# Two more staging places and two more places for decoded pieces of w_in, in memory that is not yet in use, with the order searched anew

## The chip, the core and the metric

The kernel runs on one core of a Trainium2 chip. The metric is the device time of one execution in microseconds (us). The engines are TensorE (PE, with its weight loads PEld), VectorE (DVE), ScalarE (ACT), GpSimd (POOL) and SyncE (SP), which here only issues DMAs.

## What is computed

An attention with two parts, and behind it a gated feed-forward layer. There are 8 batches, 8 heads, 576 positions of 64 values.

```
q_d, k_d, v_d = mean of 4 neighbouring positions          # 144 positions
x  = softmax(q_d k_d^T / 8) v_d, each row repeated 4 times
   + softmax(q k^T / 8 where |i - j| < 4, else -1e9) v    # a band
x  = heads side by side: 576 x 512 per batch
h  = relu(x @ w_in);  u, v = h[:, :512], h[:, 512:]       # w_in 512 x 1024
v  = (v - mean) / sqrt(var + 1e-6)
vs = w_spatial @ v + b_spatial                            # 576 x 576
out = (u * vs) @ w_out                                    # w_out 512 x 512
```

The inputs q, k, v, w_spatial and b_spatial are float32; w_in and w_out come as 64-bit floats.

## The kernel before

**How the work is tiled.** Heads go in pairs, 4 pairs per batch and 32 in all; `attention(n)` issues the steps of one pair, `gated(b)` those of one batch's feed-forward part. The steps have short names that the prediction uses. S: the banded scores of a pair (L748), on ten windows of 64 queries; the mask is added either by a product on PE ahead of it (L741) or on DVE (L761). Sd: the scores of the coarse attention (L810), of sums over 4 positions that DVE or POOL make (L720, L723). T and Td: both probabilities turned over on PE (L844, L891). AV and AVd: the products with v (L952, L919). Then DVE adds the two (tile xf, L971, L973), ACT rounds the sum to 16 bits (x high, L1002) and DVE stores what is left (x low, L1004). Between these, DVE takes the maxima (L764, L770; coarse L852 to L854), subtracts them (L767, L776) or scales them for ACT to subtract (L780), and adds up and inverts the sums (L794 to L801, L862, L866); ACT takes the exponentials. Which engine takes a step that could go to two is set by strings of letters, one letter per pair (`ON`).

V is x @ w_in's second half (L1029, the last 64 positions L1034), for five pieces of 128 positions: ACT applies the relu, DVE the statistics and the scaling, and the result is stored as a high and a low half in the tile vh. U is w_in's first half turned (L1092): eight pieces per batch, four for positions 0 to 255 and four for the rest. SP (not to be mixed up with the engine) is the product with w_spatial (L1124), also eight pieces; DVE multiplies each with its U (the gate, L1145) and the product is stored as high and low half in a tile of the tag g (L1130, L1135), of which there are three, ga and two in gb. O is the product with w_out (L1160, L1175). Every float32 operand of these products is a sum of two 16-bit halves, so each product takes three passes.

**The weights.** w_in and w_out come in eight and four pieces of 128 rows x 512 numbers of 64 bits, 512 KB each (L522). A piece is staged as it came in a place of the tag stg (four places, two in the tile stg, which lies where gb will be, two in more), decoded to float32 by ACT (L539) and DVE (L542, L547) into a place of the tag mb (six places), measured by ACT (L648), and, when all pieces of a matrix half are measured and the common scale is known (L479 to L503), split into two 16-bit halves by ACT (L510) and DVE (L513). WV is w_in's second half, WU its first. A place is free again when its last reader has run.

**What sets the order.** Nothing here is scheduled by hand. All steps are collected as operations with an engine, an assumed duration and the tiles that they read, write or hold; `Plan.run` then plays the program through and takes, at each step, the engine that could start first and on it the operation of the smallest rank among those that can start within `NEAR` of the first. The rank is the pair's or batch's number plus an offset from the tables `RANK`, `MRANK` and `WRANK`. The tables, `NEAR`, `STAY`, `EVICT` and the strings of `ON` are thus what the order hangs on. Each engine then runs its instructions in that order. Where the played time has a hole on PE in the first 110 us, filler matmuls are put in (L1204), which keep PE's clock up and whose result nobody reads.

Of the kernel before, what the change touches and what calls it, by code (L numbers as in the profile page):

```python
# [252 lines left out]
RANK = {"load": [143.005, 47.751, 252.982, -69.47, -172.22, -274.786, 560.411, -758.364, -311.459, 313.434, 266.06, 380.575,  # L253
            943.336, 399.915],
        "vload": [391.404, 86.345, 272.249, 337.531, 429.684, -52.69, -370.895, -252.053],
        "vabs": [509.637, -1181.093, -217.316, 87.185, -457.776, 123.004, -794.489, 144.366],
        "tv": [-183.93, 240.18, 765.617, 930.011, 56.071, -19.127, -157.242, 125.859],
        "sum": [-115.268, 142.997, -94.455, -372.167, 362.55, -75.596, 306.456, 702.576, 1696.966, 425.169, -234.075, 705.288,
            -421.357, 223.437],
        "S": [-1061.927, -157.575, 379.809, -830.223, -915.099, 670.631, 141.564, -649.896, 467.386, 88.454, 513.148, 238.256,  # L260
            245.41, 202.772],
        "E": [-534.894, -339.729, -702.236, 21.188, 160.003, 471.872, 219.972, 899.326, -409.142, -823.461, -265.585, -479.069,
            -503.017, -440.633],
        "N": [231.109, -483.572, -754.504, 524.152, -141.085, 397.308, 1325.226, -80.846, -320.013, -220.077, -64.133, -498.673,
            700.859, -253.394],
        "T": [-347.227, -440.539, -1149.413, -139.403, 917.828, -1374.545, -1166.794, 234.909, 536.972, -105.532, -561.257,
            -49.343, -383.904, -24.157],
        "Sd": [-228.884, 341.247, -989.571, 12.731, -290.563, 65.584, -210.501, 584.996, 760.783, -156.288, -493.755, 182.161,
            -206.462, -81.893],
        "Nd": [20.186, -634.328, -625.655, -47.029, -1024.698, 6.919, -369.885, -166.975, -196.395, -51.441, 745.233, 26.68,  # L270
            590.548, 680.939],
        "Td": [226.557, -226.969, 765.057, -163.935, 412.294, -360.224, 842.794, -998.859, 11.321, 28.445, -152.942, 58.045,
            -1153.807, -259.463],
        "AVd": [377.528, -777.682, -319.581, 176.718, 599.105, 1049.442, -339.489, -191.118, -286.676, -150.229, -415.778,
            -182.501, -118.84, 141.634],
        "AV": [60.151, -170.544, -717.724, 720.142, -836.725, 275.504, 440.562, -339.226, -949.724, 57.757, -184.347, -239.42,
            -4.966, -560.047],
        "X": [49.462, -601.369, 382.04, -619.469, -420.239, 803.995, 16.415, -27.426, 201.671, 266.124, -288.114, 118.52,
            -424.608, -87.751]}
MRANK = {"V": [[-120.813, 103.137], [-373.166, -785.223], [-588.287, 86.439], [-457.053, -295.554], [-271.069, 53.075],  # L280
            [-161.929, 7.172], [-384.75, 67.584], [1.753, -86.54]],
        "U0": [[-381.018, 507.475], [-225.844, -398.15], [392.079, 353.99], [415.277, -261.891], [-69.09, -16.703], [-362.251,
            -497.795], [59.314, -190.411], [573.297, -308.684]],
        "S0": [[631.14, 127.639], [-206.013, -184.383], [299.174, 561.899], [-372.357, 30.262], [381.875, 239.103], [33.324,
            19.169], [-136.587, -125.569], [104.744, -531.737]],
        "U1": [[66.951, 205.966], [432.921, 80.243], [202.58, -320.842], [-584.875, -261.385], [85.111, -539.421], [-290.079,
            -515.53], [-73.151, -407.568], [-105.893, -362.577]],
        "O0": [[170.632, -34.982], [-172.469, 696.573], [159.95, -390.053], [-841.668, -359.026], [22.932, -667.87], [-349.956,
            231.605], [321.827, -73.48], [-54.093, -578.395]],
        "S1": [[-122.247, -1002.997], [272.521, 179.124], [-502.627, -34.942], [83.425, -28.324], [193.115, 251.294], [212.725,  # L290
            -514.576], [-0.655, 14.458], [254.101, -410.908]],
        "O1": [[-425.021, 297.386], [239.962, 469.652], [56.568, -208.235], [-194.872, 129.628], [-641.125, -6.104], [281.584,
            274.929], [184.644, 89.516], [19.298, 376.248]]}
EVICT = 456.633
WRANK = {"WV load": [31.22, -21.921, 242.309, 4.474],
        "WV decode": [350.543, -287.444, -567.367, 661.466],
        "WV bound": [-83.736, 162.235, 909.503, 36.755, -835.361],
        "WV split": [-201.598, 11.031, -341.826, -1007.43],
        "WU load": [-364.293, 427.826, 390.089, -59.831],
# [950 lines left out]
```

## Time and profile before

| | us |
|---|---|
| median of 3 runs | 579.53 |
| lowest and highest run | 578.91, 579.99 |
| the profiled execution | 580.97 |
| its span, first to last instruction | 579.1 |
| PE busy | 551.6 (95%) |
| DVE busy | 414.1 (72%) |
| ACT busy | 376.3 (65%) |
| POOL busy | 186.7 (32%) |
| HBM read, written | 46.57 MB, 9.44 MB |

The profile gives a start and a duration for each instruction, and for each idle time what ended it. Neighbours on an engine overlap a little, so that what one instruction costs in a row of them is the distance of two starts, 0.05 to 0.1 us less than its duration. A stretch of the span is read by how busy each engine is in it; the mean over the span hides that.

### The profile page before, as it was taken

What the parts mean: (1) busy time and instruction counts of PE and PEld (TensorE: products, weight loads), DVE (VectorE), ACT (ScalarE), POOL (GpSimd) and SP (SyncE); (2) the same over time, 40 slices, a digit from 0 to 9 for tenths busy, and PEclk for the clock granted to TensorE, in tenths of its full rate; (3) what the DMA queues carried; (4) which work ended last, traced back from release to release, by engine and by line L of the source; (5) the groups of instructions that cost most, each with busy time, mean ns of one, the idle gap of its engine ahead of it and who ended that gap; (6) DMA issues with size and microseconds to landing.
All of it is one profiled execution on the core that took longest, in us unless ns stands there. A gap on an engine that the chain in (4) does not pass through costs nothing.

```text
span 579.1 us, 16048 instructions
## 1 busy us (share of the span) xinstructions
PE 551.6 (95%) x6501; PEld 368.0 (64%) x6501; DVE 414.1 (72%) x1084; ACT 376.3 (65%) x1076; POOL 186.7 (32%) x213
## 2 busy tenths in 40 slices
PE   5877899999999998999999999999999999999996
PEld 2445547764786566765776747778567567756752
DVE  5989899964898888578687776781976666844420
ACT  3689999457577677567575877565756665954422
POOL 3636533023531254154330432422422352202100
PEclk9999999999999999999999999999999999999999
DMA  8987870035322344225303343214220400010012
GB/s 285 338 241 213 215 180 1 1 102 143 88 83 91 115 103 126 65 90 138 86 20 119 99 113 102 84 65 108 77 100 2 138 2 19 8 32 1 20 54 74
DMA packets 37390, 57.04 MB, mean 99 GB/s; under 512 B 3650, under 2 KB 24130, under 8 KB 37316
## 3 DMA queue, kind: packets, MB, share of 16 engines
q1 hardware_dynamic: 35012, 48.94, 26.7%
q0 software_dynamic: 2304, 7.08, 7.2%
q8 instruction: 51, 0.84, 0.6%
q14 instruction: 23, 0.19, 0.1%
HBM read 46.57 MB, written 9.44 MB: 97 GB/s over the span
## 4 chain that ended last, share of the span: by engine, by line
PE 70%; DVE 18%; ACT 6%; issue 2%; DMA 2%; POOL 0%; SPq 0%; ACTq 0%; DVEq 0%; POOLq 0%
PE pmd L1124 4%; PE pma L1124 4%; PE pmb L1160 4%; PE pma L1160 4%; PE pmc L1029 4%; PE pmc L1160 4%; PE pma L1029 4%; PE pmc L1124 3%; PE pmb L1124 3%; PE pmd L1029 3%; PE pmd L1092 2%; PE pma L1092 2%; PE pmc L1092 2%; PE pmb L1029 2%; PE pmd L1160 2%
## 5 line engine op out<-in xcount | busy, mean ns | idle before, releaser
L1092 PEld LDWEIGHTS <-win 128*128 128x128 f16 x768 | 74.7, 98 | 20.8 <-issue 0.6
L1124 PEld LDWEIGHTS <-vha 128*128 128x128 f16 x768 | 74.0, 98 | 20.6 <-issue 2.1
L1160 PEld LDWEIGHTS <-gb 128*128 128x128 f16 x264 | 25.6, 98 | 28.5 <-issue 0.4
L1124 PE MATMUL pma<-wsp,vha 128*128 128x256 f16 (+1 forms) x216 | 29.4, 286 | 0.0
L1124 PE MATMUL pmd<-wsp,vha 128*128 128x256 f16 (+1 forms) x204 | 27.6, 285 | 1.3 <-DVE aua L1105 1.3
L1204 PE MATMUL pma<-mask_b,mask_a 128*128 128x512 bf16 x83 | 23.4, 415 | 3.1 <-DVE mask_a L383 3.1
L1124 PE MATMUL pmb<-wsp,vha 128*128 128x256 f16 (+1 forms) x180 | 24.1, 283 | 0.0
L1124 PE MATMUL pmc<-wsp,vha 128*128 128x320 f16 (+1 forms) x168 | 23.5, 290 | 0.0
L1160 PE MATMUL pmb<-wo,gb 128*128 128x512 f16 x96 | 22.0, 379 | 0.0
L1160 PEld LDWEIGHTS <-ga 128*128 128x128 f16 x120 | 11.6, 98 | 12.8 <-issue 0.2
L1057 POOL TENSOR_TENSOR sta<-sta,mhalf 128x1 f32<-128x1 f32 (+1 forms) x14 | 9.0, 646 | 32.3 <-DVE sta L1041 32.3
L669 POOL DMA_DIRECT2D tvb<-v_dram x12 | 10.8, 900 | 18.2 <-DMA tvb<-v_dram 15.7
L1160 PE MATMUL pma<-wo,gb 128*128 128x512 f16 x72 | 16.5, 379 | 0.0
L1029 PEld LDWEIGHTS <-xa 128*128 128x128 f16 x96 | 9.2, 98 | 10.8 <-issue 0.2
L1204 PEld LDWEIGHTS <-mask_a 128*128 128x128 bf16 x85 | 7.9, 104 | 12.6 <-issue 3.7
L720 POOL TENSOR_TENSOR suma<-qka 128x576 f32<-128x576 f32 x6 | 7.8, 1294 | 23.4 <-DMA qka<-qk_dram 23.4
L669 POOL DMA_DIRECT2D tva<-v_dram x12 | 10.8, 902 | 13.2 <-DMA tva<-v_dram 8.9
L1057 POOL TENSOR_TENSOR stb<-stb,mhalf 128x1 f32<-128x1 f32 (+1 forms) x15 | 10.9, 725 | 11.4 <-DVE stb L1041 11.4
L1160 PE MATMUL pmc<-wo,gb 128*128 128x512 f16 x60 | 13.8, 379 | 0.0
L1057 POOL TENSOR_TENSOR stc<-stc,mhalf 128x1 f32<-128x1 f32 (+1 forms) x11 | 7.5, 678 | 18.7 <-DVE stc L1041 15.2
L720 POOL TENSOR_TENSOR sumb<-qkb 128x576 f32<-128x576 f32 x6 | 7.8, 1296 | 16.5 <-DMA qkb<-qk_dram 16.5
L862 POOL TENSOR_SCALAR smdb<-smdb 112x3 f32<-112x3 f32 x3 | 0.6, 201 | 38.6 <-ACT eda L858 38.6
(1085 smaller groups left out, 1725.7 us busy)
## 6 DMA issues: line engine op xcount, KB each, us to landing
qka<-qk_dram SPq DMA_DIRECT2D x15, 576.0 KB, 4.9
qkb<-qk_dram SPq DMA_DIRECT2D x15, 576.0 KB, 6.2
tva<-v_dram POOLq DMA_DIRECT2D x12, 288.0 KB, 5.5
tvb<-v_dram POOLq DMA_DIRECT2D x12, 288.0 KB, 4.3
stg<-w_in_dram SPq DMA_DIRECT2D x5, 512.0 KB, 8.3
out_dram<-rowc SPq DMA_DIRECT2D x7, 256.0 KB, 2.2
out_dram<-rowb SPq DMA_DIRECT2D x7, 256.0 KB, 2.0
out_dram<-rowe SPq DMA_DIRECT2D x7, 256.0 KB, 2.1
```

The costliest lines, as they stand in the source:

```text
L669: plan.op("POOL", 850, lambda r=r: nc.gpsimd.dma_start(t.ap[LOW:KEYS], v4[b, r], accum_op=ALU.add), w=[t], rank=rank + 2.0 + 0.3 * r, kb=2 ...
L720: side(s1).tensor_tensor(sb.ap.rearrange("p x (g r) -> p x g r", r=2), x[:, :, :, :2], x[:, :, :, 2:], op=ALU.add)
L862: side(ivd).tensor_scalar(smd.ap[:PD], smd.ap[:PD], 1.0e-9, 4.0, op0=ALU.add, op1=ALU.mult)
L1029: nc.tensor.matmul(ps.ap, xs[c].ap[:, i, t * P:(t + 1) * P], win[:, c, j, FF:], start=(c == 0 and (i, j) == (0, 0)), stop=(c == NC - 1 and ...
L1057: plan.op("POOL", 530, lambda: nc.gpsimd.tensor_tensor(st.ap[:r, 8:9], st.ap[:r, 8:9], mhalf[:r], op=ALU.pow), w=[st], rank=rank - EVICT, ...
L1092: nc.tensor.matmul(ps.ap[:, :n], win[:, c, i, ft * P:(ft + 1) * P], xs[c].ap[:, j, HA[h]:HA[h + 1]], start=(c == 0 and (i, j) == (0, 0)), ...
L1124: nc.tensor.matmul(ps.ap[:, :n], vh.ap[:, c, i, fs], wsp[:, c, j, hs], start=(c == 0 and (i, j) == (0, 0)), stop=False)
L1160: nc.tensor.matmul(ps.ap, g.ap[:, c, HA[1] * i + k:HA[1] * i + k + P], wo[:, c, j, :], start=(c == 0 and (i, j) == (0, 0)), stop=(c == NF ...
L1204: nc.tensor.matmul(ap.rearrange("p (j k) -> p j k", k=64), mask_a, mask_b[:, None, :].broadcast_to([P, 8, 64]), start=True, stop=True)
```

## The change

Two tiles are added in memory that is used for something else later. `extra` (two staging places, tag stv) lies where vh, the normalised v, will be; the first two pieces of WU are staged there. `spare` (two places for decoded pieces, tag mbx) lies where ga, the first gated tile, will be; the last two pieces of WU are decoded into it. vh and ga are made when they are first needed, as gb already was. So w_in's eight pieces have six staging places and eight places for their decoded form. Two conditions follow: V of the first batch waits for all that use the places of stv, and the first SP for all that use those of mbx. All tables of the order have new numbers.

```diff
-RANK = {"load": [143.005, 47.751, 252.982, -69.47, -172.22, -274.786, 560.411, -758.364, -311.459, 313.434, 266.06, 380.575,
+RANK = {"load": [193.743, 24.538, 296.961, -103.771, 2.185, -58.429, 515.387, -691.613, -313.739, 439.058, 82.64, 215.719,
...
-NEAR = 104.496
-STAY = 26.882
+NEAR = 101.451
+STAY = 32.658
...
-ON = {"sub": "DDDDDDADDADAAADDDADDAAADDDA",
+ON = {"sub": "AADDDDAAAAADAAADDADAADAADDDDDDAD",
...
-        "mask": "TTTTTTTTD",
-        "norm": "PDPPPDPDPPDDDPDPPPDPDPDPPPPDDPD",
+        "mask": "DTTTTTTDTD",
+        "norm": "PDPPPDPPDDPDPPPDPDDDDDPDDPPDDDPD",
...
-    plan.tag("g", [const.tile([P, NF, 2 * HA[1]], F16, name="ga"), g_place(0), g_place(1)])
+    spare = const.tile([P, 2, FF], F32, tag="ga", name="spare")
+    plan.tag("mbx", [spare[:, 0], spare[:, 1]])
+    plan.tag("g", [lambda: const.tile([P, NF, 2 * HA[1]], F16, tag="ga", name="ga"), g_place(0), g_place(1)])
...
-    places("vh", 1, [P, NT, 2, FF], F16)
+    extra = const.tile([P, 2, 2 * FF], F32, tag="vh", name="extra")
+    plan.tag("stv", [extra[:, 0], extra[:, 1]])
+    plan.tag("vh", [lambda: const.tile([P, NT, 2, FF], F16, tag="vh", name="vha")])
...
-        t = fetch([(src, 0)], key, 1600)
-        eb, mb = plan.buf("row"), plan.buf("mb")
+        t = fetch([(src, 0)], key, 1600, "stv" if key in (("WU", 0), ("WU", 1)) else "stg")
+        eb, mb = plan.buf("row"), plan.buf("mbx" if key in (("WU", 2), ("WU", 3)) else "mb")
...
+    def users(tag):
+        return [o for o in weights if any(b.tag == tag for b in o.bufs)]
...
-                plan.op("PE", 12 * 216, mm, r=xr + wtok["WV"], w=[ps], hold=[vr, vh], rank=rank, lag=PEL + 60, mode="F", name="V")
+                plan.op("PE", 12 * 216, mm, r=xr + wtok["WV"], w=[ps], hold=[vr, vh], after=users("stv") if b == 0 else (), rank=rank, lag=PEL + 60, mode="F", name="V")
...
-            first = weights if (b, h) in ((0, 1), (1, 0)) else ()
+            first = weights if (b, h) in ((0, 1), (1, 0)) else users("mbx") if b == 0 else ()
```

What the numbers do to the order can be seen where the instructions stand. The line numbers of the new kernel are 3 to 8 higher.

SP's queue, the first DMAs of the program; `stg`, `more` and `extra` take pieces of w_in, `qka` to `qkd` the queries and keys of the first four pairs, `tva` the coarse v. Before:

```order
L667 DMA tva<-v_dram 72x1024
L522 DMA stg<-w_in_dram 128x1024 x2
L713 DMA qka<-qk_dram 128x1152
L713 DMA qkb<-qk_dram 128x1152
L522 DMA more<-w_in_dram 128x1024 x2
L713 DMA qkc<-qk_dram 128x1152
L713 DMA qkd<-qk_dram 128x1152
L522 DMA wsta<-wT_dram 128x576
L522 DMA biasa<-bsp_dram 2x576
```

In the new order:

```order
L526 DMA extra<-w_in_dram 128x1024
L674 DMA tva<-v_dram 72x1024
L526 DMA stg<-w_in_dram 128x1024 x2
L720 DMA qka<-qk_dram 128x1152
L720 DMA qkb<-qk_dram 128x1152
L526 DMA more<-w_in_dram 128x1024 x2
L720 DMA qkc<-qk_dram 128x1152
L720 DMA qkd<-qk_dram 128x1152
L526 DMA extra<-w_in_dram 128x1024
L526 DMA wsta<-wT_dram 128x576
```

One piece stands ahead of everything, another behind qkd; the four that came first stand as they did.

ACT's queue, where WU is split (`win<-mb...` and `win<-spare`; `xe` is the first x of the second batch, `edb` a coarse exponential, `rowd`, `rowa` and `rowc` are V's relu). Before:

```order
L1047 ACTIVATE rowd<-pmb,sx2a 128x512
L686 ACTIVATE junk,sxb<-va 128x640
L510 ACTIVATE win<-mbf,sw 128x512
L510 ACTIVATE win<-mbc,sw 128x512
L1047 ACTIVATE rowa<-pma,sx2a 128x512
L510 ACTIVATE win<-mbd,sw 128x512
L539 ACTIVATE rowe<-stg 128x512
L686 ACTIVATE junk,sxa<-vb 128x640
L1047 ACTIVATE rowc<-pmd,sx2a 128x512
L510 ACTIVATE win<-mbe,sw 128x512
L1002 ACTIVATE xe<-xfb,sxb 128x576
```

In the new order:

```order
L901 COPY pdTa<-pmc 100x288
L543 ACTIVATE rowc<-more 128x512
L514 ACTIVATE win<-mbf,sw 128x512
L514 ACTIVATE win<-mbe,sw 128x512
L865 ACTIVATE edb,smdb<-paa,mxdb 112x2x72
L865 ACTIVATE edb,smdb<-pmb,mxdb 112x2x72
L865 ACTIVATE edb,smdb<-paa,mxdb 112x2x72
L514 ACTIVATE win<-spare,sw 128x512 x2
L693 ACTIVATE junk,sxb<-ve 128x640
L853 COPY probTb<-paa 128x640
```

The four splits stood among the relus of V, so behind the first batch's last x; now they stand among the steps of the first batch's attention, ahead of every x.

DVE's queue at the last split of w_out (`wo<-mb...`; `uf`, `ug`, `uh` are gates of the first batch, `xf` its row sums of the second). Before:

```order
L836 TENSOR_TENSOR sb<-sb,smd 128x640
L513 SCALAR_TENSOR_TENSOR wo<-mbb,sw,wo 128x512
L513 SCALAR_TENSOR_TENSOR wo<-mba,sw,wo 128x512
L971 TENSOR_TENSOR xfa<-paa,dnb 128x2x116 x2
L973 TENSOR_TENSOR xfa<-paa,dnb 128x112
L482 TENSOR_REDUCE aua<-pmd 1x1
L483 TENSOR_SCALAR aua<-aua 1x1
L513 SCALAR_TENSOR_TENSOR wo<-mbf,sw,wo 128x512
L513 SCALAR_TENSOR_TENSOR wo<-mbc,sw,wo 128x512
L1004 SCALAR_TENSOR_TENSOR xf<-xfa,sxb,xf 128x576
```

In the new order:

```order
L859 TENSOR_REDUCE mxda<-pab 112x2
L860 TENSOR_REDUCE mxda<-pmc 112x1
L861 TENSOR_SCALAR mxda<-mxda 112x3
L1142 TENSOR_TENSOR ga<-uf,ga 128x256
L1152 SCALAR_TENSOR_TENSOR ug<-pmd,aua,ug 128x256
L517 SCALAR_TENSOR_TENSOR wo<-mbb,sw,wo 128x512
L801 TENSOR_REDUCE smd<-sc 128x10
L933 TENSOR_TENSOR dnb<-paa,dnb 128x144
L804 TENSOR_SCALAR smd<-smd 128x10
L808 RECIPROCAL smd<-smd 128x10
L1152 SCALAR_TENSOR_TENSOR uh<-pma,aua,uh 128x256
```

The four splits stood close together ahead of the first gate; the last one now stands behind two gates, with the steps of two pairs around it.

## Rows read from the trace of the kernel before

**Rows 1.** The busy time of each engine in six stretches of the whole program (stretch in us, its length, busy us and count of instructions by engine, granted clock, share of the DMA engines, GB/s).

```profile
0.00:12.91 12.91, 6.45 (x59) 2.77 (x59) 7.86 (x18) 3.94 (x7) 3.62 (x18) 1.00 0.84 269
12.91:40.93 28.02, 22.67 (x293) 12.86 (x297) 23.26 (x57) 18.77 (x55) 14.11 (x15) 0.94 0.95 287
40.93:72.42 31.49, 25.24 (x537) 16.61 (x527) 29.57 (x78) 30.55 (x88) 18.39 (x19) 1.00 0.82 229
72.42:106.17 33.75, 32.04 (x263) 20.83 (x262) 32.62 (x88) 30.16 (x73) 9.77 (x11) 1.00 0.32 78
106.17:134.40 28.23, 28.23 (x365) 18.93 (x365) 22.94 (x64) 15.35 (x45) 7.20 (x6) 1.00 0.28 90
134.40:579.10 444.70, 436.98 (x5002) 295.99 (x5000) 297.80 (x783) 277.55 (x812) 133.58 (x144) 1.00 0.27 75
```

**Rows 2.** The timeline of PE at the end of the program, its last matmuls (start, us, what, how many in a row).

```profile
571.36 2.75 PE L1175 MATMUL pmd<-wo,gta 128*128 128x512 f16 x12
```

**Rows 3.** The waits of PE from 72 to 575 us, the first and the last of seven (us in total, times, longest).

```profile
PE pmd L1124 <- DVE aua L1105: 1.3, 1, 1.3
...
PE pma L1092 <- DVE win L513: 0.2, 1, 0.2
```

**Rows 4.** The busy time of line 1204 alone (the filler matmuls) over stretches that make up the whole span, their sum.

```profile
sum 579.10, PE 24.04 PEld 7.94; mean PE 4.81 PEld 1.59
```

**Rows 5.** DVE in the first 106.17 us, its busy time and number of instructions, and two of its waits there, the longest behind the first decodes and the shortest of the eight.

```profile
0.00:106.17 106.17, 93.31 (x239) 0.98 0.70 201
...
DVE mxb L770 <- PE pab L748: 1.6, 1, 1.6
...
DVE sxa L482 <- PE pmb L479: 0.2, 1, 0.2
```

**Rows 6.** The chain of waits in the first 125 us (start, us, what).

```profile
2.59 10.28 DMA qkb<-qk_dram
...
104.00 1.32 DVE wo L513 x2
...
106.17 1.79 PE pmd L1124 x12
...
110.14 0.55 PE pab L844 x5
```

**Rows 7.** The timeline of ACT and, below it, of DVE in the first 80 us (start, us, line, out<-in).

```profile
5.84 0.66 ACT L539 ACTIVATE rowa<-stg 128x512 f32<-128x512 f32 x1 [3.82 <-DMA stg<-w_in_dram]
...
44.40 0.67 ACT L539 ACTIVATE rowb<-more 128x512 f32<-128x512 f32 x1
...
77.81 0.73 ACT L510 ACTIVATE win<-mbf,sw 128x512 f16<-128x512 f32 x1
...
9.67 0.75 DVE L720 TENSOR_TENSOR suma<-qka 128x576 f32<-128x576 f32 x1
...
40.93 0.74 DVE L513 SCALAR_TENSOR_TENSOR win<-mbd,sw,win 128x512 f16<-128x512 f32 x1
```

**Rows 8.** The timeline of PE, one masked block of scores in the opening and the five steps of one pair later on.

```profile
70.78 0.43 PE L741 MATMUL pab<-mask_b,mask_a 128*128 128x320 bf16 x2
...
209.03 0.72 PE L919 MATMUL pab<-pdTa,tvb 64*64 64x144 f32 x16
209.58 0.80 PE L952 MATMUL pab<-probTa,vf 64*64 64x60 f32 x38
...
211.45 0.49 PE L891 MATMUL pma<-perm,edb 112*100 112x112 f32 x3
...
212.07 0.49 PE L1092 MATMUL pmd<-xb,win 128*128 128x256 f16 x3
```

**Rows 9.** The timeline of DVE ahead of the second batch's V.

```profile
131.00 0.89 DVE L761 TENSOR_TENSOR sa<-pab,mask 128x384 f32<-128x384 f32 x2
131.92 0.82 DVE L764 TENSOR_REDUCE mxb<-sa 128x10 f32<-128x640 f32 x1
...
132.86 0.81 DVE L1004 SCALAR_TENSOR_TENSOR xa<-xfa,sxb,xa 128x576 f16<-128x576 f32 x1
133.58 0.45 DVE L852 TENSOR_REDUCE mxdb<-pab 112x2 f32<-112x288 f32 x1
...
134.28 0.17 DVE L854 TENSOR_SCALAR mxdb<-mxdb 112x3 f32<-112x3 f32 x1
```

**Rows 10.** Groups of DVE's instructions in the first 106.17 us (busy us, mean ns of one), and below them two rows of the timelines of DVE and POOL that overlap.

```profile
L720 DVE TENSOR_TENSOR suma<-qka 128x576 f32<-128x576 f32 x2 | 3.2, 1577 | 0.0
L542 DVE TENSOR_SCALAR mba<-rowa 128x512 int32<-128x512 int32 x2 | 1.9, 956 | 0.7 <-ACT rowa L539 0.7
L854 DVE TENSOR_SCALAR mxda<-mxda 112x3 f32<-112x3 f32 x2 | 1.8, 892 | 0.1
L513 DVE SCALAR_TENSOR_TENSOR wsp<-wstc,sw,wsp 128x576 f16<-128x576 f32 x1 | 1.7, 1705 | 0.0
...
L542 DVE TENSOR_SCALAR mbc<-rowc 128x512 int32<-128x512 int32 x2 | 0.8, 416 | 0.0
...
26.81 2.40 DVE L720 TENSOR_TENSOR suma<-qka 128x576 f32<-128x576 f32 x1
...
27.45 1.14 POOL L720 TENSOR_TENSOR sumb<-qkb 128x576 f32<-128x576 f32 x1
```

**Rows 11.** The timeline of PE at the first V of the second batch.

```profile
134.23 0.81 PE L1029 MATMUL pmc<-win,xe 128*128 128x512 f16 x3
```

More of the change, by code (lines that the diff above doesn't have):

```diff
@@ L247, in run @@
         return end
-RANK = {"load": [143.005, 47.751, 252.982, -69.47, -172.22, -274.786, 560.411, -758.364, -311.459, 313.434, 266.06, 380.575,
[L254 to L299, printed above, removed]
-        "WU decode": [387.574, -316.232, 1019.795, 459.568],
-        "WU bound": [1425.684, -228.293, 245.85, 118.051, 725.352],
-        "WU split": [-187.848, -607.313, -258.771, -328.661],
-        "WSP load": [289.708, -579.107, 622.627, -316.354, 744.76],
-        "WSP bound": [397.382, 106.669, -930.598, 200.751, 873.332, -382.338],
-        "WSP split": [-150.625, -91.686, 309.424, 430.824, -1165.74],
-        "WO load": [201.774, -325.888, 429.457, 987.307],
-        "WO decode": [137.835, 619.019, -225.889, -8.083],
-        "WO bound": [-64.148, 457.463, -289.1, 18.247, -58.582],
-        "WO split": [620.04, -563.746, 894.059, 1022.164]}
@@ new lines @@
+EVICT = 424.128
+WRANK = {"WV load": [8.932, -69.308, 237.335, -113.461],
+        "WV decode": [498.39, -173.71, -746.769, 879.963],
+        "WV bound": [75.164, 328.117, 1096.662, 290.394, -1001.895],
+        "WV split": [-246.43, 101.682, -127.118, -970.709],
+        "WU load": [-496.994, 344.788, 640.584, 37.355],
+        "WU decode": [469.162, -148.932, 1081.304, 729.559],
+        "WU bound": [1666.078, -368.299, 333.39, 481.782, 710.79],
+        "WU split": [-307.465, -783.187, -230.312, -132.514],
+        "WSP load": [481.299, -741.394, 761.131, -123.43, 725.764],
+        "WSP bound": [-211.952, 408.604, -994.87, 166.184, 872.953, -437.445],
+        "WSP split": [-58.134, -137.272, 55.809, 426.781, -1354.283],
+        "WO load": [130.61, -93.203, 516.501, 829.072],
+        "WO decode": [15.979, 664.366, -112.237, 34.148],
+        "WO bound": [-19.709, 334.246, -466.101, 68.581, 19.425],
+        "WO split": [888.478, -529.737, 813.101, 1132.568]}
@@ L320 @@
 UPN = 0
[L322 to L329 removed]
+ON = {"sub": "AADDDDAAAAADAAADDADAADAADDDDDDAD",
+        "inv": "DDDDDDPDDDPDPDDDDPDPDPDDDPDDPPD",
+        "invd": "DDDPDDDPDPPPDDDDDPPPDDPPPDPDDDPD",
+        "sum": "PPPPPDDDDPDDPPPDDPDPDDPPPPDDDDPD",
+        "mask": "DTTTTTTDTD",
+        "norm": "PDPPPDPPDDPDPPPDPDDDDDPDDPPDDDPD",
+        "normd": "PAAPDDAAAPAAPDDAPDADDDPADPDPAAAP",
+        "vlo": "DPDDPDDPDPDPDDDDPPDDPDPDDDPDPDPPDPDP"}
 @with_exitstack
```

45 lines of the change are left out of this document (40 added, 5 removed).

## The prediction, made before the changed kernel ran

> **What bounds the kernel now.** I read the page's 40 slices first, then the engines' busy time cut at five points, then the chain of waits, and at last single rows of VectorE (DVE) and TensorE (PE). The reader is to see two kernels in one. PE is busy nearly all the time, but the stretches differ [rows 1]: from 134.40 us to the end PE is busy 436.98 of 444.70 us, and 5.0 of the 7.7 us that are missing lie behind its last matmul [rows 2]; the waits of PE from 72 us on are seven, 1.3 us the longest and 4.2 us in sum [rows 3]. Before 72.42 us, where the first V (w_in times the first batch) starts, PE's busy time is 6.45 + 22.67 + 25.24 = 54.4 us, but 24.0 of these are filler matmuls that only keep PE awake [rows 4]. So of the first 72.4 us PE uses 30.3, and by 106.17 us, where the first gated product of the second half starts (SP of the tile called ue), it has used 86.4 - 24.0 = 62.4 and lost 43.8. After that it loses 2.5 us in four of those waits, and the tail. **The span is thus a fixed amount of PE work, 527.6 us, plus what PE loses before 106 us, 43.8, plus 7.7 us.** A new order can win or lose only by that second part, unless it opens holes behind it.
>
> What sets the second part is DVE, with ScalarE (ACT) close by. DVE is busy 93.31 of the first 106.17 us [rows 5]; of the 12.9 us that it idles, some 5 are the start and the first decodes, and eight waits behind them, 1.6 us the longest, make up 5.7. From 40.93 us, where the first split of w_in ends on ACT's side, it is busy 29.57 of 31.49 and 32.62 of 33.75 us [rows 1], and the chain runs through it up to 105 us [rows 6]: the last split of w_out (tile mbc) starts at 104.59 us there, and the SP that needs all weights starts at 106.17.
>
> **The change, part by part.** *Two staging places more.* In the new order the first DMA of SP's queue is a w_in piece (tile extra) in front of tva, stg, qka and qkb. A piece is 512 KB, and the core moves 269 GB/s in the first 12.9 us and 287 in the 28 us behind [rows 1]. So whatever stands behind it lands 512 KB / 287 to 269 GB/s = 1.8 to 1.9 us later: the first decode (5.84 us, after 3.82 us of waiting), and qkb, whose landing at 12.87 us opens the chain [rows 6, 7]. In return all eight w_in pieces are decoded before the third pair's scores are exponentiated; before, ACT decodes the seventh at 44.40 us [rows 7]. The bytes of the first 41 us are nearly the same, at a DMA share of 0.84 to 0.95 [rows 1], so a piece that goes early pushes another back.
>
> *Two decoded places more.* w_in's first half (for U) is bound and split before the first x is finished; before, that was done from 77.81 us on, beside the running V [rows 7]. In the new order four more splits stand ahead of the last x of the batch on DVE, each 0.74 us [rows 7]. That work is not saved, it is moved from a place where PE was saturated to a place where PE waits for DVE.
>
> *The two waits that come with it.* The first V waits until two staged pieces are decoded, the first SP until two decoded pieces are split. Both stand on DVE ahead of the last x of the batch, which V waits for anyway. Behind them on PE queue V, U and SP, but the price is nothing as long as the x come last; if that cover went, a split's 0.74 us would show [rows 7]. The filler matmuls go from 85 to 95 in the program; they run in holes and cost nothing, or 0.28 us each where one is in the way (24.04 us for 85) [rows 4].
>
> *The order.* I count DVE's and PE's work up to the same event in both kernels: the SP of ue, which must have the last w_out split. On PE the new order has done more by then: one S, Sd, AV and T and two Td and AVd more, and one mask product less. The pair at 209.03 us shows AVd, AV, S, Sd and Td in 212.07 - 209.03 = 3.04 us, Td takes 0.62 of them and AVd 0.55, T is 0.55 in the chain and a mask product 0.43 [rows 6, 8]: 3.04 + 0.55 + 0.62 + 0.55 - 0.4 = 4.4 us. This is no loss, it would be done later.
>
> On DVE the new order has done still more by the last w_out split. From start to start of the rows where they stand in line [rows 7, 9]: sums of two pairs more, 2 x (0.75 and, over half as many elements, 0.4) = 2.3; masks of two pairs that PE masked before, 2 x 0.9 = 1.8; one maximum more, 0.8; three pairs fewer whose maximum is subtracted on DVE (ACT's exponential does it now; like the mask it passes over all scores), -3 x 0.8 = -2.4, with four small scalings, +0.3; one more pair of coarse maxima, 0.8 (133.58 to 134.45), and of inverses, 0.7; one norm less and one coarse norm more, +0.2; one dn, xf and xlo more, 0.2 + 0.8 + 0.7 = 1.7; one v-low more, 0.6; the gate's scale, two gates and one low part before the last split instead of behind it, 1.6. What has no row of its own here I size by the rows of like form. Sum 8.4 us. The bounds: 7 if the small ones run beside others, 9.4 if they are slowed as often as before.
>
> So DVE is later by 8.4 us and PE by only 4.4 us of useful work: PE loses **4.0 us** more, if DVE idles as long as before. Does it? The opening is worse by the 1.8 us of the extra piece; the eight waits of DVE behind that, 5.7 us in sum [rows 5], can shrink, since more decoding stands ready to fill them. Stepping through the first 40 us by these rows I get the first w_in split about 1 us earlier with 1.1 us less work ahead of it: no gain in idle time. I take idle as unchanged and keep -5.7 and +1.8 as bounds. From the V on, the count by PE gives the same: by the last x, DVE has 2.4 us more to do (four splits, less a column reduction and some subtractions), PE has 4.0 us less behind it, of which 1 to 3 us can come back since U and V are now mixed; that is +3.4 to +6.4.
>
> Behind that point: the same PE work less one mask product (0.36), one round more of switches between attention and projections; I set this to nothing. The four waits of 2.5 us [rows 3] may go or come anew. The tail is alike: the last product, two copies, two stores.
>
> **Sum.** The profiled execution took 580.97 us with a span of 579.1; the median of the three runs is 579.53, 1.4 below it. Span 579.1 + 4.0 = 583.1, execution 585.0; against the median **583.5 us**.
>
> **Rivals.** (1) *DVE is held up less.* In the first 106 us some DVE rows take far longer than their like while GpSimd (POOL) runs: two sums of suma 3.2 us where one alone takes 0.75, two rows of mba 1.9 where mbc's take 0.8, two of mxda 1.8 where one can take 0.17, a split of wsp 1.7 where one of w_in takes 0.74 [rows 7, 9, 10]; 1.7 + 1.1 + 1.4 + 0.9 = 5.1 us together. The new order meets POOL otherwise. If none of them came back, DVE's 8.4 would be 3.3, and PE would lose 5.1 less than in my sum: 578.4. For it: by the order POOL has three normalisations fewer in all. Against: it has two sums more, and suma was hit by just such a sum. The Trainium skill, SBUF — State Buffer, "Who interferes with whom", says that a VectorE instruction with two SBUF inputs and a GpSimd instruction that reads SBUF take turns on one port, whichever starts first; by that rule the slow sum of suma (26.81 to 29.21 us) waits for POOL's sum at 27.45 to 28.59, and the trace agrees, since the two overlap and the DVE row ends 0.6 us behind the other [rows 10]. Chance of ending faster 0.12.
>
> (2) *The gaps are filled.* If the early decodes took all of the 5.7 us of DVE waits, less the 1.8 us of the late opening, DVE would be 3.9 us ahead of my sum: 579.6, no change. With one or two slowed rows fewer it is faster. Chance 0.23, a third of it faster.
>
> (3) *The second batch's V stalls* (slower still). Before, its last x is done at 133.67 us [rows 9] and V starts at 134.23 [rows 11]: nothing to spare. In the new order PE has 7.2 us less work ahead of that V (counted from the order as above), so it comes there at 134.2 - 7.2 + 4.0 = 131.0, while DVE has 1.1 us more work ahead of that x. DVE idles 28.23 - 22.94 = 5.3 us between 106 and 134 [rows 1]. If that idle time stays, the x is done at 134.8 and PE stalls 3.8 us more: 587.3. If it goes, x is done at 129.5 and nothing happens. It decides as long as less than all 3.8 us of that idle time goes. Against it: AV of that pair now stands 5.3 us of PE work ahead of the V, and the chain behind it took 3.8. Chance 0.20.
>
> (4) *The pieces come no earlier*, because DMA is full. Then the decodes wait on ACT in front of the exponentials, and the opening costs its 1.8 us as well: 585.3. It lies within my forecast's own range.
>
> **How the numbers follow.** My forecast (with 4) covers +1.2 to +6 us: 0.45. Rival 3: 0.20. Rivals 1 and 2 together 0.35, of which 0.20 faster and 0.15 within 0.2% (1.2 us, about what a measurement of this kernel can tell from no change). Faster 0.20, same 0.15, slower 0.65. The range reaches down past rival 1, 577.5, and up past rival 3, 588.0.
>
> **What would show it.** Right: the last w_out split some 8 us later than 104.6, the SP of ue at 114 to 116 us, DVE 95% busy between 41 and 112 us, PE without a hole from then on. The first V at 73 to 76 us with one pair's scores fewer done. Wrong: that SP before 111 us (DVE idles less or meets POOL less), or later holes in PE of more than 6 us, which would be the searched order's own and not this sum's.

## The result and the profile after

The changed kernel takes 583.7 us (median of 4 runs, 583.16 to 584.3) where the kernel before takes 579.7 in the same four rounds: ratio 1.0071, 95% interval 1.0054 to 1.0089, so 4 us slower. The profiled execution took 583.63 us, its span is 581.9.

The same six stretches as in [rows 1], of the kernel after:

```profile
0.00:12.91 12.91, 7.70 (x60) 3.07 (x60) 6.04 (x16) 3.95 (x7) 5.26 (x20) 1.00 0.85 280
12.91:40.93 28.02, 20.56 (x262) 11.65 (x263) 22.30 (x50) 21.01 (x72) 14.85 (x16) 0.94 0.92 291
40.93:72.42 31.49, 24.29 (x456) 15.23 (x457) 30.63 (x94) 30.13 (x84) 6.49 (x7) 1.00 0.78 213
72.42:106.17 33.75, 31.73 (x322) 20.31 (x322) 32.19 (x82) 31.37 (x80) 13.74 (x16) 1.00 0.37 85
106.17:134.40 28.23, 28.23 (x449) 20.77 (x441) 25.92 (x79) 21.58 (x77) 1.89 (x2) 1.00 0.30 95
134.40:581.90 447.50, 441.21 (x4977) 298.79 (x4975) 291.23 (x776) 269.24 (x770) 133.83 (x146) 1.00 0.26 74
```

The busy time of the filler matmuls alone (the line that is 1204 in [rows 4]), up to the first V and behind it, and their sum:

```profile
0.00:72.42 72.42, 26.02 (x95) 9.10 (x95) 0.98 0.84 255
72.42:581.90 509.48, 0.22 (x2) 0.00 (x0) 1.00 0.27 76
sum 581.90, PE 26.24 PEld 9.10; mean PE 13.12 PEld 4.55
```

The timeline of PE: the first V of the first batch, the SP of ue, the first V of the second batch ([rows 6, 11] have the last two before):

```profile
72.48 0.81 PE L1036 MATMUL pmb<-win,xa 128*128 128x512 f16 x3
...
115.71 1.79 PE L1131 MATMUL pmb<-wsp,vha 128*128 128x320 f16 x12
...
132.28 0.81 PE L1036 MATMUL pmd<-win,xe 128*128 128x512 f16 x3
```

The timeline of ACT in the opening, as in [rows 7]; line 543 is the first step of a decode, line 795 the exponential that ACT takes window by window:

```profile
7.89 0.66 ACT L543 ACTIVATE rowa<-stg 128x512 f32<-128x512 f32 x1 [5.88 <-DMA stg<-w_in_dram]
...
15.44 0.66 ACT L543 ACTIVATE rowc<-more 128x512 f32<-128x512 f32 x1 [3.40 <-DMA more<-w_in_dram]
16.00 2.48 ACT L795 ACTIVATE sa<-sa,mxa 128x64 f32<-128x64 f32 x10
18.51 2.16 ACT L795 ACTIVATE sb<-pab,mxb 128x64 f32<-128x64 f32 x10
...
30.03 0.69 ACT L543 ACTIVATE rowc<-stg 128x512 f32<-128x512 f32 x1
```

The timeline of DVE: a sum that is held up, the first w_in split, the last x of the batch, the last w_out split:

```profile
34.18 1.81 DVE L727 TENSOR_TENSOR sumb<-qkb 128x576 f32<-128x576 f32 x1
...
43.44 0.74 DVE L517 SCALAR_TENSOR_TENSOR win<-mbd,sw,win 128x512 f16<-128x512 f32 x1
...
72.26 0.81 DVE L1011 SCALAR_TENSOR_TENSOR xd<-xfa,sxa,xd 128x576 f16<-128x576 f32 x1
...
114.40 0.74 DVE L517 SCALAR_TENSOR_TENSOR wo<-mbb,sw,wo 128x512 f16<-128x512 f32 x1
```

DVE's waits up to there, the longest and two on these exponentials (us in total, times, longest):

```profile
DVE mba L546 <- ACT rowa L543: 2.8, 1, 2.8
...
DVE sma L801 <- ACT sa L795: 1.2, 1, 1.2
DVE smb L801 <- ACT sb L795: 1.2, 2, 0.7
```

POOL beside the sum that is held up:

```profile
34.06 1.32 POOL L843 TENSOR_TENSOR sa<-sa,sma 128x640 f32<-128x640 f32 x1 [2.14 <-DVE sma L808]
```

Busy time up to the end of the last w_out split (columns as above):

```profile
0.00:115.13 115.13, 93.23 (x1279) 57.54 (x1280) 99.28 (x262) 93.71 (x268) 42.22 (x59) 0.99 0.67 193
```

What to see. V starts where it did, 72.48 against 72.42 us, but PE has used only 52.55 - 26.02 = 26.5 us by then instead of 30.3: some 4 us of attention work are left for later. By the SP of ue (115.71 us, 9.5 later than in [rows 6]) PE has used 52.55 + 31.73 + 9.54 - 26.24 = 67.6 us and lost **48.1**, against 43.8 before. Behind that SP it loses 6.3 us where it lost 7.7, because the span is 581.9 and PE's useful work unchanged (553.71 - 26.24 = 527.5 us). Together +2.8 us of span; the rest of the 4 us is that the profiled execution of before lay 1.4 above its median, and this one does not.

### The profile page after: what moved, and what is told of

The parts are those of the page before. It is cut to its first block, busy times and chain, and to the rows that moved or that the text cites. A ratio compares the mean times of both kernels' runs of the same rounds, so it can differ in the third digit from the quotient of the medians.

```text
span 581.9 us, 16082 instructions
## 1 busy us (share of the span) xinstructions
PE 553.7 (95%) x6509; PEld 369.8 (64%) x6509; DVE 408.3 (70%) x1091; ACT 377.3 (65%) x1085; POOL 176.1 (30%) x205
## 4 chain that ended last, share of the span: by engine, by line
PE 76%; DVE 10%; ACT 7%; DMA 3%; issue 1%; SPq 1%; ACTq 0%; DVEq 0%
PE pmd L1131 5%; PE pma L1131 5%; PE pmd L1036 4%; PE pmc L1099 4%; PE pmd L1167 4%; PE pmb L1099 4%; PE pma L1099 4%; PE pma L1036 3%; PE pma L1167 3%; PE pmd L1099 3%; PE pmb L1131 3%; PE pmc L1131 3%; PE pmc L1167 3%; PE pmb L1036 3%; PE pmb L1167 2%; PE pmc L1036 2%
## 5 line engine op out<-in xcount | busy, mean ns | idle before, releaser
L1131 PE MATMUL pmd<-wsp,vha 128*128 128x256 f16 (+1 forms) x252 | 33.6, 283 | 0.4 <-ACT edb L865 0.4
L1131 PE MATMUL pma<-wsp,vha 128*128 128x320 f16 (+1 forms) x228 | 31.9, 289 | 0.0
L1131 PE MATMUL pmc<-wsp,vha 128*128 128x256 f16 (+1 forms) x144 | 19.6, 286 | 0.0
L1131 PE MATMUL pmb<-wsp,vha 128*128 128x320 f16 (+1 forms) x144 | 19.6, 286 | 0.0
L1167 PE MATMUL pmd<-wo,gb 128*128 128x512 f16 x84 | 19.3, 379 | 0.0
L1211 PEld LDWEIGHTS <-mask_a 128*128 128x128 bf16 x95 | 9.1, 105 | 14.5 <-issue 5.2
L1167 PE MATMUL pmc<-wo,gb 128*128 128x512 f16 x72 | 16.5, 379 | 0.0
L869 POOL TENSOR_SCALAR smdd<-smdd 112x3 f32<-112x3 f32 x5 | 1.3, 260 | 39.1 <-ACT edb L865 39.0
L1064 POOL TENSOR_TENSOR stb<-stb,mhalf 128x1 f32<-128x1 f32 (+1 forms) x12 | 8.9, 741 | 13.3 <-DVE stb L1048 11.2
L1045 DVE BATCH_NORM_STATS2 stc<-rowc 128x6 f32<-128x512 f32 x3 | 2.1, 693 | 13.4 <-ACT rowc L1054 13.4
## 6 DMA issues: line engine op xcount, KB each, us to landing
stg<-w_in_dram SPq DMA_DIRECT2D x4, 512.0 KB, 12.3
```

What stands on the lines that cost most here:

```text
L869: side(ivd).tensor_scalar(smd.ap[:PD], smd.ap[:PD], 1.0e-9, 4.0, op0=ALU.add, op1=ALU.mult)
L1045: nc.vector.bn_stats(st.ap[:r, :6], vr.ap[:r])
L1064: plan.op("POOL", 530, lambda: nc.gpsimd.tensor_tensor(st.ap[:r, 8:9], st.ap[:r, 8:9], mhalf[:r], op=ALU.pow), w=[st], rank=rank - EVICT, ...
L1131: nc.tensor.matmul(ps.ap[:, :n], vh.ap[:, c, i, fs], wsp[:, c, j, hs], start=(c == 0 and (i, j) == (0, 0)), stop=False)
L1167: nc.tensor.matmul(ps.ap, g.ap[:, c, HA[1] * i + k:HA[1] * i + k + P], wo[:, c, j, :], start=(c == 0 and (i, j) == (0, 0)), stop=(c == NF ...
L1211: nc.tensor.matmul(ap.rearrange("p (j k) -> p j k", k=64), mask_a, mask_b[:, None, :].broadcast_to([P, 8, 64]), start=True, stop=True)
```

## The experiments

In the runs on the order, one part of the new order is undone and every other instruction of every engine stays where it was, the fillers too. "V" is the start of the first V in the run's profiled execution, "behind V" that execution's time less V, "first split" the start of the first split of w_in on DVE. The medians, and the ratios to the kernel before in the same rounds (its median there lies between 579.47 and 579.84) with their 95% intervals:

| run | median us | ratio | first split | V | behind V |
|---|---|---|---|---|---|
| the kernel after | 583.70 | 1.0071 (1.0054 to 1.0089) | 43.44 | 72.48 | 511.2 |
| late_extra | 582.05 | 1.0038 (1.0023 to 1.0053) | 41.52 | 70.55 | 511.4 |
| no_exp_by_window | 582.92 | 1.0061 (1.0039 to 1.0082) | 41.98 | 71.01 | 511.8 |
| opening_both | 582.64 | 1.0047 (1.0035 to 1.0059) | 41.65 | 70.68 | 512.1 |
| no_splits | 582.19 | 1.0048 (1.0032 to 1.0064) | 43.12 | 70.86 | 512.0 |
| no_splits_late_extra | 581.06 | 1.0025 (1.0013 to 1.0036) | 41.67 | 69.42 | 511.6 |
| late_splits | 586.32 | 1.0109 (1.0091 to 1.0128) | 43.45 | 71.16 | 515.8 |
| splits_spread | 586.74 | 1.0114 (1.0098 to 1.0130) | 43.49 | 71.25 | 515.5 |
| all_three | 586.35 | 1.0107 (1.0092 to 1.0123) | 42.02 | 69.77 | 516.7 |
| the kernel before | 579.7 | 1 | 40.93 | 72.42 | 508.6 |
| places_alone | 579.44 | 0.9997 (0.9984 to 1.0011) | 39.42 | 70.88 | 508.5 |
| dve_price | 582.38 | 1.0047 (1.0034 to 1.0061) | 39.65 | 73.81 | 508.2 |
| act_price | 583.79 | 1.0064 (1.0040 to 1.0088) | 42.16 | 75.83 | 508.0 |
| dve_price_late | 585.48 | 1.0096 (1.0068 to 1.0124) | 39.08 | 70.56 | 512.6 |

From the first split to V the profiled executions repeat to 0.05 us: 31.46 to 31.49 us in the kernel before, places_alone and dve_price_late, 29.03 or 29.04 in the kernel after and the three runs below it in the table, 27.71 to 27.76 in the five runs without the four splits there. Ahead of it they do not. Four executions run the old order unchanged up to there (the kernel before, places_alone, dve_price, dve_price_late) and have it at 39.08 to 40.93 us. In three of them the granted clock falls to 0.50 on the way, in the kernel before from 14 to 16 us, in places_alone and dve_price from 28 to 30; in dve_price_late it stays at 1.00. So a difference of a microsecond or two in one execution's opening needs the medians beside it.

### places_alone: the new places in the old order

The diff is that of the change without its tables and letters.

> The new places and the two waits that come with them, but the order of the kernel before, instruction by instruction on every engine, with its letters and its filler matmuls. If the loss is the order's alone: as the kernel before, 579.7 us within 0.6. If the places or their waits cost something themselves: 581 us or more. If they give something by themselves (a DMA that no longer waits for a place): 578.5 or less.

579.44 us, no difference. The places, the tiles that are made late and the two added waits cost nothing and give nothing that can be told from zero (the interval is -0.9 to +0.6 us); the loss is the order's. The run shows one thing more. Its first w_in split, its first V and its SP of ue, in the old order, stand at (timelines of DVE and PE)

```profile
39.42 0.74 DVE L621 SCALAR_TENSOR_TENSOR win<-mbd,sw,win 128x512 f16<-128x512 f32 x1
...
70.88 0.82 PE L1140 MATMUL pmb<-win,xa 128*128 128x512 f16 x3
...
104.64 1.79 PE L1235 MATMUL pmd<-wsp,vha 128*128 128x320 f16 x12 [1.34 <-DVE aua L1216]
```

and dve_price_late, whose order up to V is also the old one, has V at 70.56. The profiled execution of before, with 72.42, was one with a late opening, by 1.5 to 1.9 us, about what it lies above its median. The delay arises early: the second pair's scores, which wait for qkb, start at 12.91 us there and run at a falling clock,

```profile
12.91 1.16 PE L748 MATMUL pab<-qkb 64*64 64x64 f32 x40 [2.07 <-DMA qkb<-qk_dram]
```

against 11.66 us and 0.81 for them in places_alone.

### late_extra: the extra piece later

```diff
 SP's queue
-L526 DMA extra<-w_in_dram 128x1024
 L674 DMA tva<-v_dram 72x1024
...
 L720 DMA qkd<-qk_dram 128x1152
+L526 DMA extra<-w_in_dram 128x1024
 L526 DMA extra<-w_in_dram 128x1024
```

> The changed kernel in its own order, with one edit: the first piece in the tile extra is issued on SP's queue behind qkd, next to the second one, instead of ahead of everything. Theory A (the extra piece delays the opening by the 1.8 us that it takes): first decode at about 6 us instead of 7.89, DVE idle of the first 25 us from 11.2 to about 9.4 us, time 581.9 us. Theory B (that idle time comes from the exponentials that ACT now takes window by window in the first two pairs): the opening's end does not move, 583.7 us within 0.5.

582.05 us, 1.65 less than the kernel after, as theory A had it. ACT's first decode starts at 5.34 instead of 7.89:

```profile
5.34 0.67 ACT L647 ACTIVATE rowa<-stg 128x512 f32<-128x512 f32 x1 [3.33 <-DMA stg<-w_in_dram]
```

and V starts 1.9 us earlier with the same work ahead of it, all of which is won ahead of the first w_in split:

```profile
41.52 0.74 DVE L621 SCALAR_TENSOR_TENSOR win<-mbd,sw,win 128x512 f16<-128x512 f32 x1
```

Other executions agree: with the piece in front and the opening otherwise as in the kernel after, that split starts at 43.12 to 43.49 (four), with the piece late at 41.52 and 41.67 (two). The piece that went ahead was not needed first: ACT decodes it fifth.

### no_exp_by_window and opening_both

```diff
-ON = {"sub": "AADDDDAAAAADAAADDADAADAADDDDDDAD",
+ON = {"sub": "DDDDDDAAAAADAAADDADAADAADDDDDDAD",
```

> The changed kernel in its own order, with one edit: for the first two pairs DVE subtracts the maximum and ACT takes one exponential (0.7 us each), instead of ACT's ten small ones per pair (2.48 and 2.16 us). Theory A (DVE idles in the opening because it waits for these): ACT has 3.2 us less in the opening, DVE 1.2 us more in time in which it idled; 582.0 to 583.0 us. Theory B (DVE's work counts one to one whatever it waits for): 584.9 us.

> Both edits of the opening in the changed kernel: the first piece in the tile extra behind qkd on SP's queue, and one exponential instead of ten for each of the first two pairs. If the two take away different idle time, their gains of 1.65 and 0.8 us add up: 581.2 us, DVE's idle time of the first 25 us near 6 us instead of 11.2. If they share it: 582.0 us.

The first gives 582.92, and its interval does not tell it from the kernel after. Both edits together, 582.64, are no better than the late piece alone. Busy times of the first 25 us, of the kernel after and, below it, of opening_both:

```profile
0.00:25.00 25.00, 15.98 (x182) 7.45 (x183) 13.74 (x30) 13.12 (x40) 12.99 (x28) 0.94 0.94 324
```

```profile
0.00:25.00 25.00, 17.56 (x190) 7.95 (x191) 19.69 (x40) 10.79 (x25) 13.70 (x29) 0.93 0.93 326
```

DVE's idle time falls from 11.3 to 5.3 us, as much as hoped for, and V comes no earlier (70.68). So idle time of DVE in the first 25 us is no measure of what is lost in the opening: up to the first w_in split DVE is busy 33.67 us in opening_both and 31.04 in late_extra, and the split starts at 41.65 and 41.52. ACT was relieved of 2.3 us in the first 25 us. Why none of that shows in the time is open; the granted clock, one candidate, was 0.50 in two stretches of opening_both (22 to 24 and 36 to 38 us) and in one of late_extra (20 to 22).

### late_splits, splits_spread, all_three: the splits put back behind x

```diff
 ACT's queue (late_splits; DVE's four low splits move likewise)
-L514 ACTIVATE win<-mbf,sw 128x512
-L514 ACTIVATE win<-mbe,sw 128x512
-L514 ACTIVATE win<-spare,sw 128x512 x2
...
 L865 ACTIVATE eda,smdc<-pab,mxdc 112x2x72
+L514 ACTIVATE win<-mbf,sw 128x512
+L514 ACTIVATE win<-mbe,sw 128x512
+L514 ACTIVATE win<-spare,sw 128x512 x2
```

In splits_spread they stand one by one behind V's relu (L1054), v's measure (L693), the next relu and the bias' measure, and the first U goes behind the third V; all_three is that with the two edits of the opening.

> The changed kernel in its own order, with one edit: the four splits of w_in's first half (four ACT, four DVE instructions) stand behind the first batch's last x on ACT and DVE instead of among its attention steps. Theory A (the prediction's sum: what counts is DVE's work up to the last w_out split, and that is unchanged): V starts up to 2.8 us earlier, but PE then waits that much in front of the SP of ue; 583.7 us, within 0.7. Theory B (what counts is what stands ahead of the first V): V 2.8 us earlier and no new wait, 580.9 us.

> The changed kernel with the four splits of w_in's first half behind the first batch's last x, but spread out: on ACT each behind an instruction that TensorE waits for, and the first U one V later, so that the 3.2 us wait of the run with the splits in a row should not come. Theory B (what stands ahead of V counts): the 1.3 us by which V starts earlier stay: 582.4 us. Theory A (DVE's and ACT's work up to the last w_out split counts, and is unchanged): given back in a wait behind V, 583.7 us or more.

> The last two together: the late piece, one exponential per pair in the opening, and the splits spread out behind the last x. If the loss against the kernel before is made of these three (1.65 + 0.8 + 1.3 us): 580.0 us, within 0.5 of the kernel before. If the splits' part is given back: 581.2 us.

All three are slower than the kernel after, by 2.6 to 3.0 us. Neither theory had that for late_splits and all_three (all_three is 3.7 above opening_both, which differs from it by the splits alone); for splits_spread it lies in theory A's "or more", which gave no size. V does start 1.2 to 1.3 us earlier in the first two. But ACT's queue is then 2.5 us behind (four splits), and PE's next instruction after two V needs one of ACT. The waits of PE in late_splits, the longest, and four stretches around it:

```profile
PE pma L587 <- ACT junk L797: 3.2, 1, 3.2
```

```profile
77.00:80.25 3.25, 0.05 (x1) 0.00 (x0) 3.18 (x8) 3.22 (x9) 0.79 (x2) 0.85 0.01 3
80.25:83.00 2.75, 2.75 (x81) 2.50 (x81) 1.89 (x8) 2.70 (x6) 2.75 (x4) 0.50 0.03 9
83.00:86.00 3.00, 3.00 (x20) 1.87 (x15) 0.97 (x5) 0.78 (x3) 1.90 (x3) 0.50 0.83 157
86.00:89.00 3.00, 3.00 (x19) 1.77 (x19) 2.79 (x13) 1.99 (x6) 0.88 (x1) 0.98 0.93 261
```

The wait costs 3.2 us, and then again: the granted clock is 0.50 (1.2 GHz) from 80.25 to 86, where PE, at half its clock, does in 5.75 us the work of 2.9. In splits_spread the longest wait is 2.5 us, with two of 0.7 and 0.5 beside it:

```profile
PE paa L740 <- DVE xfb L1084: 2.5, 1, 2.5
```

There ACT's third split ends late, DVE's low split waits 0.8 us for it and takes 1.06, and xf's sums, which PE waits for, stand behind that one. So the place behind V, where PE has V and U to do, had no room on ACT and DVE.

### no_splits and no_splits_late_extra: the splits left out

```diff
-                lambda: nc.vector.scalar_tensor_tensor(dst_lo, src(), scale, dst_hi, op0=ALU.mult, op1=ALU.subtract),
+                lambda: key[0] == "WU" or nc.vector.scalar_tensor_tensor(dst_lo, src(), scale, dst_hi, op0=ALU.mult, op1=ALU.subtract),
...
-    nc.tensor.matmul(ps.ap[:, :n], win[:, c, i, ft * P:(ft + 1) * P], xs[c]
+    nc.tensor.matmul(ps.ap[:, :n], win[:, c, i, FF + ft * P:FF + (ft + 1) * P], xs[c]
```

The line of ACT's high split is edited in the same way. The second run has late_extra's move too.

> The changed kernel without the splits of w_in's first half (four ACT and four DVE instructions that stand ahead of the first batch's last x are left out; U reads the split pieces of the second half instead, so its values are not those wanted). Nothing else moves. Theory A (DVE's work counts one to one): DVE 2.9 us less ahead of V and behind it nothing more, 580.9 us. Theory B (only what the runs with moved splits showed at V, 1.3 us): 582.4 us. If these splits stand in idle time: 583.7 us.

> The same without the splits of w_in's first half, and with the first piece in the tile extra behind qkd on SP's queue. If these two are the loss against the kernel before and add up: 583.7 - 2.9 - 1.65 = 579.2 us. If they bring V forward by the same stretch, or another engine sets the end there: 581 to 582 us.

582.19 us: the four splits of DVE and the four of ACT cost some 1.5 us where they stand, not the 2.9 that they last. Its interval and that of the kernel after overlap a little, but the traces point the same way: from the first w_in split to V it is 27.74 us here and 29.04 in the kernel after, 1.3 less. V:

```profile
70.86 0.81 PE L1036 MATMUL pmb<-win,xa 128*128 128x512 f16 x3
```

With the late piece it is 581.06, 2.6 less than the kernel after and 1.0025 times the kernel before (1.0013 to 1.0036); within the noise the two add up (1.5 + 1.65 = 3.15). V:

```profile
69.42 0.81 PE L1140 MATMUL pmb<-win,xa 128*128 128x512 f16 x3
```

### dve_price, act_price, dve_price_late: the price of work in the old order

```diff
dve_price (act_price: the same for the high split on ACT)
+        def low():
+            for _ in range(2 if key[0] == "WV" else 1):
+                nc.vector.scalar_tensor_tensor(dst_lo, src(), scale, dst_hi, op0=ALU.mult, op1=ALU.subtract)
dve_price_late
+        late_wo = key == ("WO", 3)
...
+            for _ in range(6 if late_wo else 1):
+                nc.vector.scalar_tensor_tensor(m, lo, 29, m, op0=ALU.logical_shift_right, op1=ALU.bitwise_or)
```

> The kernel before with DVE's four low splits of w_in's second half computed twice: 4 x 0.74 = 2.96 us more DVE work between 41 and 55 us, nothing else moved. If DVE's work ahead of V counts one to one (the step of the prediction's sum): 582.7 us. If it counts as the four splits of w_in's first half did, 1.3 of 2.8: 581.1 us. If other engines set the end there: 579.7 us.

> The kernel before with ACT's four high splits of w_in's second half computed twice: 4 x 0.62 = 2.5 us more ACT work between 40 and 45 us, nothing else moved. If ACT is as much a bound as DVE there: 582.0 us. If it has room (it idles 3.2 of the 33.75 us behind V): 580.0 us or less.

> The kernel before with the last step of the decoding of w_out's last piece done six times instead of once: 5 x 0.6 = 3.0 us more DVE work at 91.5 us, behind V and all splits of w_in, ahead of the last w_out split. The prediction's sum (DVE's work up to the last w_out split counts, wherever it stands): 582.7 us. If only work ahead of the first V counts, because PE has V and U to do: 579.7 to 580.5 us.

2.96 us more on DVE ahead of V cost 2.7 us (2.0 to 3.5 by the interval): one to one, or a little less; from the first w_in split to V it is 2.7 us more than in places_alone, too. 2.5 us more on ACT cost 3.7 us (2.3 to 5.1): ACT is as much the bound as DVE there. V in act_price:

```profile
75.83 0.82 PE L1032 MATMUL pmb<-win,xa 128*128 128x512 f16 x3
```

It is 5 us later than in places_alone, but 2 of these lie ahead of the edit: ACT's first split starts at 40.65 instead of 38.63. From that split to V the price is 2.9 us, part of it waits of DVE for the doubled splits (0.6 us twice).

The last step of the decoding, done six times behind V, cost 5.6 us (3.9 to 7.2; the runs scatter from 583.13 to 587.71, and the profiled one is among the lowest, at a granted clock of 0.997 where the two longest have 0.987). It was meant as 3.0 us more DVE work; in the profiled execution the six take 5.15 us where the one takes 0.68 in the kernel before, so 4.5 more. So this work behind V is not covered by PE's either. The decoded piece comes late, ACT's measure of it waits, and behind it in ACT's queue stand U's relus, which PE waits for. The two waits of PE and the clock after them (0.50 from 97 to 100 us):

```profile
PE pmb L479 <- ACT junk L651: 2.5, 1, 2.5
PE pmd L1095 <- ACT ub L1098: 0.9, 1, 0.9
```

```profile
92.00:95.00 3.00, 1.11 (x9) 0.59 (x6) 2.90 (x5) 0.16 (x1) 0.00 (x0) 1.00 0.00 0
95.00:98.00 3.00, 1.49 (x7) 0.79 (x8) 2.93 (x8) 3.00 (x11) 0.86 (x1) 0.82 0.00 0
98.00:101.00 3.00, 3.00 (x15) 1.59 (x14) 2.97 (x5) 2.16 (x5) 1.51 (x1) 0.61 0.00 0
```

## Why the prediction was right, point by point

**The sum came out (583.5 forecast, 583.7 measured), by terms that were off in both directions.** The prediction had the whole loss as DVE's added work less PE's, and DVE's idle time unchanged. Of the loss up to the SP of ue, 4.3 us, the first gave 1.6 (6.8 less 5.2) and the idle time 3.0. So the direction was right, the cause for the most part another than forecast, and that the number came within 0.2 us is luck.

*The frame* held. PE's useful work is the same to 0.1 us, and the loss before the SP of ue grew by 4.3 us where 4.0 was forecast. What lies behind that SP did not stay alike, it fell by 1.4 us (6.3 against 7.7). That this hardly shows in the median has a reason that I had not looked for: I took 1.4 us from both kernels to come from the profile to the median, but only the execution of before that was profiled had a late opening (places_alone). Against places_alone the two errors show: the SP of ue starts 11.1 us later (104.64, 115.71) with 5.2 us more PE work done, so PE loses 5.9 us more ahead of it, not 4.0, and 1.4 less behind it, where the prediction had nothing.

*The extra piece in front* was sized right: 1.8 to 1.9 us forecast, the first decode 2.05 us later than in [rows 7], and 1.65 us of the time shown by undoing it. Of qkb, which was to land as much later, the trace of before gave a wrong picture: its scores start at 13.11 us, 0.2 later than there, but 1.4 later than in late_extra (11.76).

*"I take idle as unchanged"* is the step that failed. DVE idles 115.13 - 99.28 = 15.9 us up to the last w_out split, against 12.9 up to 106.17 [rows 5]: +3.0, beyond the upper bound of +1.8. Nearly all of it lies ahead of the first w_in split, which was worked out to come about 1 us earlier: it starts at 43.44 us, 2.5 later than in [rows 7] and 4.0 later than in places_alone, with 12.7 us of DVE idle ahead of it instead of 9.8. The early decoding did not fill the waits; the late first decode (2.8 us of waiting, 0.7 in the kernel before) and the exponentials taken window by window (1.2 and 0.5 up to that split) opened new ones. Of these two only the first is shown to cost time (late_extra); the second is not (no_exp_by_window).

*DVE's work up to that split* was forecast to grow by 8.4 us. The split starts at 114.40 instead of 104.59 [rows 6], 9.8 us later; less the 3.0 us of idle time that is 6.8, just under the lower bound of 7. *PE's work* by the SP grew by 67.6 - 62.4 = 5.2, not 4.4. The net, 9.8 us for DVE against 5.2 for PE, is the 4.3 (the SP starts 0.6 us behind the end of the split now, 0.9 before [rows 6]).

*Which event counts.* The prediction counted to the last w_out split. In the new order PE does not wait there. Every edit that leaves the instructions behind V in place gives the time back at V: behind it all of them need 511.2 to 512.1 us. Between V and that SP PE idles 2.0 us, before 1.7. So V is the event to count to, which the prediction used only as a cross check (+3.4 to +6.4; by its own terms, 2.4 + 4.0 less 1 to 3, it is +3.4 to +5.4). By it the change against places_alone is: the first w_in split 4.0 us later; from there to V 2.4 less, since some 4 us of attention work on PE with its share on DVE and ACT was left for later, though the four splits add 1.3; and 2.7 more behind V (511.2 against 508.5, the work left for later less the smaller losses there). Together 4.3 us, the difference of the two medians.

*"Moved from a place where PE was saturated to a place where PE waits for DVE"* is half true. Where they now stand the four splits cost some 1.5 us. But the place that they left, or one like it, is not free: put back behind the last x they cost 2.6 to 3.0 us more than where they are, and the extra DVE work behind V in the old order cost 5.6. In both orders DVE and ACT are nearly full on both sides of V (89 to 97% busy from 40.93 to 106.17 us), and ACT more than the prediction's "close by" says (act_price).

*The two waits and the fillers at no cost*: shown for the waits (places_alone; V starts 0.2 us behind xd). The ten fillers more were not tested.

*The rivals.* (1) Less holding up by POOL: rows are held up in the new order as well, sumb takes 1.81 us where one alone takes 0.75 [rows 7] and ends 0.6 us behind POOL's row beside it, as suma did in [rows 10]; DVE's work came out 1.6 us below the forecast, so perhaps a part of it is there, but no run isolates it. (2) Gaps filled: no, idle time grew. (3) The second batch's V: it starts at 132.28 without a stall, 1.3 us behind the 131.0 that was worked out. (4) The late opening came as priced there, but not for its reason: w_in's last piece enters decoding at 30.03 us, not 44.40 [rows 7].

*The signs.* The last w_out split 9.8 us later (some 8 forecast), the SP of ue at 115.71 (114 to 116), no hole of PE behind it over 0.5 us. V came a little before the 73 to 76 us given. DVE is 95% busy from 41 to 112 us as forecast, but it is 96% there in the kernel before, so this sign tells nothing.

*What stays open.* The piece and the splits together are 2.6 of the 4.3 us that separate the kernel after from places_alone's 579.44; and as no_splits leaves work out that the old order does as well, behind V, its part is not the price of the move. The other 1.6 lie in the rest of the order, where masks, sums and gates changed places; no run takes them apart. Of the opening's 4.0 us the piece explains 1.9. No version here beats the kernel before by more than can be measured.

## What to carry to other kernels

More buffer places are worth something only if a transfer or an instruction waits for a place: measure that first by giving the places to the old order alone, which here showed in one run that they gave nothing that could be measured. When two engines are both full, count work to the event that the idle engine really waits for, and price a moved instruction on both sides of the move, with every queue behind it; a place that looks covered because one engine is busy there may be full on another. And ask of one profiled execution whether it is a typical one before its offset to the median is carried over to the changed kernel; stretches between two events that both kernels have, as from the first w_in split to V here, repeat far better than times from the start.
